# A new written order for the first tile's jobs, and other engines for the signs of six weight chunks

## Chip, core and metric

The kernel runs on one core of one Trainium2 chip. The metric is the device time of one execution in microseconds (us). Before the change it is 944.29 us, the median of 3 runs (944.16 to 944.9).

## What is computed

Pooled attention, then a gated feed-forward layer on its output. Batch 8, 8 heads, 576 positions, head size 64; k and v are averaged over groups of 8 positions, so that 72 keys are left.

```python
k_p = k.reshape(B, H, Sp, pool, D).mean(axis=3)          # pool = 8, Sp = 72
v_p = v.reshape(B, H, Sp, pool, D).mean(axis=3)
scores = scale * np.matmul(q, k_p.transpose(0, 1, 3, 2))
attn = softmax(scores)
x = (attn @ v_p), heads joined: 4608 tokens x 512
g = x @ w_gate                                            # 512 x 1536, float64 weights
out = (g / (1 + exp(-g)) * (x @ w_val)) @ w_out           # 1536 x 512
```

q, k and v are float32, the three weights float64.

## The kernel before, in words

The 4608 tokens are cut into nine tiles of 512. For a tile the feed-forward runs over 12 chunks of 128 hidden units: a gate product (G), a value product (V), tanh and gating on ScalarE and VectorE, and a projection (O) of twelve matmuls into four PSUM banks that collect all chunks. Each float32 operand is split into a high and a low part, so that three cheap matmuls stand for one exact product. From the second tile on a planner places the work by costs and due times. The first tile has an order written out by hand, and the change is about that order.

`first_tile` (L1134) goes through the names in `ORDER` (L38 to L55) and calls one job for each. Every engine executes its instructions in program order, so what `ORDER` sets is, for each engine, the sequence of its own jobs; across engines only the data and the buffers bind. The projection of the last step and the stores of the tile's output stand outside the written part; the compiler places them. A name is letters and a number. The number is a chunk of weights, a batch (0 or 1), a piece of tokens or a step.

Transfers (all from SyncE's queue, SP in the profile): Lk and Lr bring k of batch 0 and 1, Lv and Lu bring v, Lq a piece of q, Lw a chunk of weights (L209), La inputs of batch 2, T a transposition of a piece's weights (L717), through the same queue.

Attention for pieces 0 to 8 (four of the first tile, five of the second; pieces 4 and 8 have 64 tokens): S scores (TensorE), M the scores less their maximum (VectorE, L620), E exponentials (ScalarE), Na the inverse sums (VectorE), N the product with them (GpSimd), H and P the high and low half for the transposition (ScalarE, GpSimd), T, Y the product with v (TensorE), X and Z its high and low part (ScalarE, VectorE), which are the tile's x.

Sums of v: Vp and Vq (TensorE), Vm, Vo, Vs its scale (VectorE, TensorE, VectorE), R the ratios (VectorE), Vx (ScalarE), Vh, Vg (VectorE), Vf (ScalarE) its parts. Sums of k: Kp on VectorE, Kb and Kq on GpSimd.

Weights: a chunk lies as 128 x 1536 float64 numbers in a buffer, of which there are two, shared with the first k. It is turned into float32 by integer work on its halves: a shifts the low words (L215, VectorE), b puts the sign beside them (L219), c takes the magnitude of the high words (L231, ScalarE), d joins all (L235, VectorE) and so frees the buffer for the chunk after next. Then e sums (ScalarE), f (TensorE) and g (VectorE) give a scale, h and j the high halves (ScalarE), i and k the low ones (VectorE), l and m the output weights (ScalarE, GpSimd), un a table of factors (GpSimd).

Steps 0 to 14: steps 0 to 2 are chunks 0 to 2 on the tile's first 256 tokens, steps 3 to 5 the same chunks on the other 256, steps 6 to 14 chunks 3 to 11 on all 512. G and V are twelve matmuls each (L903 to L905), t the tanh (L917), u the gating (L921), v the product with the value (L927), w and y the high and low part of the result, O the projection (L939). One PSUM bank serves all G of this tile and one all V, so that G of a step waits for u of the step before, and V for y. D and ZERO are matmuls with zeros that fill time.

`w_sign` is where the second part of the change lies. Before it there are two ways: for the chunks in `SIGN_AS_INT` an integer AND on VectorE (L225), for the others a float multiplication by 2^-60 on ScalarE that leaves a signed zero (L227).

Of the kernel before, what the change touches and what calls it, by code (L numbers as in the profile page):

```python
# [14 lines left out]
ALU = mybir.AluOpType  # L15
# [19 lines left out]


ORDER = """
Lk0 Lq0 Lk1 Lv2 Lv1 Lv0 Lq1 Lw0 Kp0 Kb0 Kp1 CZ Lw1 Lr0 Lu0 S0 Vp0 M0 Lq2 Vp2 E0 Na0 S1  # L38
a0 N0 b0 Vp1 Lq3 M1 Vm0 a1 Vo0 E1 Vs0 Kq0 R0 Vx0 H0 Vh0 Vq0 b1 Vg0 S2 Lr1 Na1 Lu2 P0 S3
Lq4 Vf0 M2 N1 T0 Lq5 H1 Kq1 Vq2 E2 c0 Y0 Lu1 Na2 X0 d0 Z0 Lw2 P1 l0 Vq1 e0 M3 T1 m0 f0  # L40
c1 N2 g0 ZERO Vm1 h0 Vo1 E3 d1 H2 j0 Vs1 Lw3 P2 e1 R1 D10 Y1 Vg1 Vx1 T2 a2 X1 l1 Vh1 un0
b2 m1 Z1 D8 f1 g1 k0 S4 i0 a3 G0 h1 Lq6 j1 M4 un1 c2 V0 k1 t0 Y2 E4 d2 b3 Lw4 i1 Na3 u0
l2 N3 D8 G1 v0 X2 w0 c3 y0 m2 Z2 O0 t1 d3 H3 V1 e2 u1 Lw5 P3 v1 l3 f2 g2 e3 T3 a4 h2 f3
j2 g3 un2 i2 w1 j3 y1 h3 k2 D4 O1 b4 i3 G2 k3 a5 V2 b5 t2 Y3 c4 u2 m3 X3 v2 Vf1 Z3 d4 G3
w2 c5 y2 Lw6 un3 t3 O2 l4 d5 e4 V3 u3 Lw7 m4 l5 f4 G4 v3 g4 w3 m5 y3 j4 O3 e5 k4 V4 Na4
t4 c6 u4 N4 f5 G5 v4 g5 h4 w4 a6 S5 H4 y4 t5 un5 b6 i4 V5 Lq7 u5 P4 M5 O4 G6 v5 T4 un4
a7 w5 c7 y5 d6 E5 O5 t6 j5 u6 Lw8 S6 e6 k5 Na5 V6 h5 Lq8 M6 l6 N5 H5 i5 f6 G7 v6 E6 P5
g6 w6 h6 y6 j6 T5 a8 O6 t7 u7 un6 Na6 c8 S7 b8 b7 V7 M7 i6 G8 E7 v7 d7 w7 Y4 y7 Lw9 N6
e7 O7 t8 d8 H6 X4 u8 Lw10 m6 Y5 e8 Z4 V8 l8 k6 X5 m8 l7 Z5 c9 f7 f8 v8 m7 G9 g7 w8 g8 j7
un7 y8 j8 un8 a9 h7 V9 t9 Na7 b9 u9 N7 O8 v9 i7 k7 w9 H7 y9 G10 k8 c10 d9 h8 V10 t10  # L50
Lw11 i8 e9 u10 La0 a10 l9 f9 O9 v10 m9 g9 w10 h9 y10 j9 un9 O10 i9 b10 k9 La1 a11 G11
b11 d10 V11 t11 Pa0 l10 u11 e10 G12 v11 w11 y11 c11 m10 f10 O11 g10 t12 d11 h10 j10 u12
l11 un10 V12 k10 e11 i10 m11 La2 G13 v12 P6 w12 y12 f11 O12 t13 g11 P7 T6 u13 h11 j11 T7
k11 S8 Ln i11 un11 Pa2 V13 M8 La3 E8 G14 La4 Na8 v13 N8 w13 y13 Y6 Pa3 t14 u14 V14 X6
Pa4 H8 La5 P8 O13 v14 La6 w14 T8 y14 Z6 Pa5 Y7 Pa6 Y8 X7 Z7 X8 La7 Pa1 Z8 Pa7 A A  # L55
"""
# [36 lines left out]
def attention_then_swiglu(  # L93
# [125 lines left out]
    def w_sign(c):  # L219


        ws, high = chunks[c]["ws"], chunks[c]["high"]
        if c in SIGN_AS_INT:
            sign = ws.bitcast(U16)
            nc.vector.tensor_single_scalar(sign[:, :, 1], sign[:, :, 3], 0x8000, ALU.bitwise_and)  # L225
        else:
            nc.scalar.activation(  # L227
                ws.bitcast(F16)[:, :, 1], high.bitcast(F32), AF.Copy, scale=2.0**-60
            )
# [904 lines left out]
    def first_tile():  # L1134
# [360 lines left out]
```

## Time and profile before

| | |
|---|---|
| median of 3 runs | 944.29 us |
| the profiled execution | 944.47 us, its span 942.5 us |
| TensorE busy | 911.6 us, 97% of the span |
| VectorE, ScalarE, GpSimd busy | 635.5, 493.5, 415.1 us |
| share of TensorE in the chain that ended last | 91% |
| first tile | the first 171 us or so of the span |

The profile is of one execution. PE is TensorE, PEld its weight load, DVE VectorE, ACT ScalarE, POOL GpSimd, SP SyncE's queue, on which all transfers are issued. A timeline row gives start and length in us, engine, line, operation, output and input, and in brackets how long the engine idled before and what released it. As each engine runs in program order, a row is matched with a job's name by counting along the order.

### The profile page before, as it was taken

The page shows a single profiled execution, that of the slowest core. Times are in us where ns is not written, and L with a number is a line of the kernel's source. Part 1 is how long each engine was busy: PE and PEld are TensorE (multiplying, and loading weights), DVE is VectorE, ACT ScalarE, POOL GpSimd, SP SyncE. Part 2 cuts the span into 40 slices and gives each one's busy share as a digit, 9 for nine tenths or more (in the row PEclk, how much of TensorE's full clock was granted, in tenths as well). Part 3 has the DMA queues.
Part 4 walks back from the last instruction along what each step waited for, and adds up shares of the span by engine and source line. Part 5 has one row for each costly group of instructions (what it writes and reads, how often), then busy time and mean ns, then how long its engine had stood idle before and what let it go on. Part 6 is the DMA issues. An engine that isn't in the chain of part 4 may idle for free.

```text
span 942.5 us, 16833 instructions
## 1 busy us (share of the span) xinstructions
PE 911.6 (97%) x6512; PEld 590.5 (63%) x6512; DVE 635.5 (67%) x1145; ACT 493.5 (52%) x971; POOL 415.1 (44%) x483
## 2 busy tenths in 40 slices
PE   5789999899999999999999999999999999999997
PEld 4567545455555576567657775776577757765775
DVE  5788877787786767676866678777854584345232
ACT  2899884264555454656365545472556554323232
POOL 4533427289747854687265442562123421120111
PEclk9899999999999999999999999999999999999999
DMA  9865634346425551654155525741322332001001
GB/s 349 247 169 186 188 134 127 111 135 199 93 75 138 159 113 30 182 132 135 29 151 148 128 51 153 182 94 27 88 59 63 74 67 57 12 1 45 1 1 46
DMA packets 155536, 103.18 MB, mean 109 GB/s; under 512 B 113216, under 2 KB 141888, under 8 KB 153920
## 3 DMA queue, kind: packets, MB, share of 16 engines
q1 hardware_dynamic: 155456, 102.11, 39.2%
q8 instruction: 51, 0.84, 0.4%
q14 instruction: 29, 0.24, 0.1%
HBM read 67.63 MB, written 9.44 MB: 82 GB/s over the span
## 4 chain that ended last, share of the span: by engine, by line
PE 91%; DMA 3%; DVE 2%; ACT 1%; POOL 1%; issue 1%; SPq 0%; POOLq 0%; DVEq 0%; ACTq 0%
PE acc L939 30%; PE gv L1036 28%; PE gv L903 9%; PE gv L904 9%; PE gv L905 9%; DMA kr<-k_rows 1%; PE ps L616 1%; DMA pt<-half 1%; PE ps L740 1%; PE ps L617 1%; PE ps L741 1%; DMA k<-k_rows 1%; DMA in<-q_rows 1%; PE ps L610 1%; ACT ws L227 0%
## 5 line engine op out<-in xcount | busy, mean ns | idle before, releaser
L1306 POOL TENSOR_TENSOR hl<-hf,hh 128x512 bf16<-128x512 f32 x69 | 91.3, 1323 | 235.7 <-ACT hh L1300 235.7
L917 ACT ACTIVATE hf<-gv,un 128x512 f32<-128x512 f32 (+1 forms) x111 | 74.9, 675 | 213.4 <-PE gv L1036 145.3
L939 PE MATMUL acc<-hh,wo_l 128*128 128x512 bf16 (+1 forms) x444 | 169.2, 383 | 0.0
L939 PE MATMUL acc<-hl,wo_h 128*128 128x512 bf16 (+1 forms) x444 | 166.1, 376 | 0.4 <-POOL hl L1306 0.2
L903 PE MATMUL gv<-x,wgv_h 128*128 128x512 f16 (+1 forms) x432 | 158.8, 368 | 3.7 <-ACT x L751 1.9
L904 PE MATMUL gv<-x,wgv_h 128*128 128x512 f16 (+1 forms) x432 | 158.6, 367 | 1.3 <-DVE x L755 1.3
L905 PE MATMUL gv<-x,wgv_l 128*128 128x512 f16 (+1 forms) x432 | 158.6, 367 | 0.5 <-DVE wgv_l L268 0.5
L921 DVE SCALAR_TENSOR_TENSOR hf<-hf,gv 128x512 f32<-128x512 f32 (+1 forms) x111 | 74.2, 669 | 109.4 <-ACT hf L917 108.9
L939 PE MATMUL acc<-hh,wo_h 128*128 128x512 f32 (+1 forms) x444 | 130.5, 416 | 0.6 <-ACT hh L1300 0.4
L599 POOL TENSOR_TENSOR box<-qt,box 64x512 f16<-64x512 f32 (+1 forms) x60 | 68.9, 1149 | 119.2 <-ACT box L598 98.7
L1036 PEld LDWEIGHTS <-mixed 128*128 128x128 f16 x1026 | 99.1, 98 | 26.6 <-issue 1.5
L1036 PEld LDWEIGHTS <-wgv_h 128*128 128x128 f16 x912 | 87.8, 98 | 32.5 <-issue 1.9
L1300 ACT CAST hh<-hf 128x512 fp32r<-128x512 f32 x69 | 42.7, 618 | 115.3 <-DVE hf L927 115.3
L1036 PE MATMUL gv<-xc,mixed 128*128 128x256 f16 x684 | 93.2, 272 | 0.0
L939 PEld LDWEIGHTS acc<-hh,wo_h 128*128 128x128 f32 x444 | 76.7, 190 | 14.8 <-ACT hh L1300 0.9
L1036 PE MATMUL gv<-xc,wgv_h 128*128 128x256 f16 x456 | 80.7, 272 | 1.3 <-DVE gv L1385 1.3
L1036 PE MATMUL gv<-x,wgv_h 128*128 128x256 f16 x456 | 80.8, 273 | 0.0
L927 DVE SCALAR_TENSOR_TENSOR hf<-gv,un,hf 128x512 f32<-128x512 f32 x69 | 51.5, 746 | 39.1 <-PE gv L1036 35.7
L939 PEld LDWEIGHTS <-wo_h 128*128 128x128 bf16 x444 | 43.4, 98 | 53.9 <-issue 27.3
L905 PEld LDWEIGHTS <-wgv_l 128*128 128x128 f16 x432 | 42.2, 98 | 48.4 <-issue 1.8
L904 PEld LDWEIGHTS <-wgv_h 128*128 128x128 f16 x432 | 42.2, 98 | 45.1 <-issue 4.4
L903 PEld LDWEIGHTS <-wgv_h 128*128 128x128 f16 x432 | 42.7, 99 | 41.4
(170 smaller groups left out, 1791.5 us busy)
## 6 DMA issues: line engine op xcount, KB each, us to landing
ws<-w_all SPq DMA_DIRECT2D x12, 1536.0 KB, 7.4
qt<-q_twice SPq DMA_DIRECT2D x48, 256.0 KB, 2.9
out_t<-ob SPq DMA_DIRECT2D x36, 256.0 KB, 2.3
in<-k_rows SPq DMA_DIRECT2D x12, 576.0 KB, 4.7
in<-q_rows SPq DMA_DIRECT2D x12, 576.0 KB, 4.8
in<-v_main SPq DMA_DIRECT2D x12, 512.0 KB, 5.0
in<-v_rest SPq DMA_DIRECT2D x12, 512.0 KB, 4.9
qt<-q_rows SPq DMA_DIRECT2D x8, 256.0 KB, 3.9
```

What stands on the lines that cost most here:

```text
L599: nc.gpsimd.tensor_sub(o[rows], qt[rows], o[rows])
L610: nc.tensor.matmul(o, qt[rows, j, :n], ksum[b][rows, j], start=True, stop=True)
L903: nc.tensor.matmul(o, wh, x["h"][:, j, a:e], start=(j == 0), stop=False)
L904: nc.tensor.matmul(o, wh, x["l"][:, j, a:e], start=False, stop=False)
L905: nc.tensor.matmul(o, wl, x["h"][:, j, a:e], start=False, stop=(j == NJ - 1))
L917: nc.scalar.activation(hf, gate, AF.Tanh, scale=un[:, c, 0:1])
L921: nc.vector.scalar_tensor_tensor(out=hf, in0=hf, scalar=1.0, in1=gate, op0=ALU.add, op1=ALU.mult)
L927: nc.vector.scalar_tensor_tensor(out=out, in0=val, scalar=un[:, c, 2:3], in1=hf, op0=ALU.mult, op1=ALU.mult)
L939: nc.tensor.matmul(acc[j][:, a:e], w[:, c, j * P : (j + 1) * P], h[:, :n], start=begin and at < NJ, stop=end and w is wo_l,)
L1036: nc.tensor.matmul(o, a, b, start=begin and j + n == 0, stop=j == HJ - 1 and n == 2, skip_group_check=True,)
L1300: nc.scalar.copy(hh[:, :n], hf)
L1306: eng.tensor_sub(hl[:, :n], hf, hh[:, :n].bitcast(F32))
```

## The change

It touches `ORDER`, which keeps its 469 names and moves some, and `w_sign`.

```diff
-Lk0 Lq0 Lk1 Lv2 Lv1 Lv0 Lq1 Lw0 Kp0 Kb0 Kp1 CZ Lw1 Lr0 Lu0 S0 Vp0 M0 Lq2 Vp2 E0 Na0 S1
-a0 N0 b0 Vp1 Lq3 M1 Vm0 a1 Vo0 E1 Vs0 Kq0 R0 Vx0 H0 Vh0 Vq0 b1 Vg0 S2 Lr1 Na1 Lu2 P0 S3
-Lq4 Vf0 M2 N1 T0 Lq5 H1 Kq1 Vq2 E2 c0 Y0 Lu1 Na2 X0 d0 Z0 Lw2 P1 l0 Vq1 e0 M3 T1 m0 f0
-c1 N2 g0 ZERO Vm1 h0 Vo1 E3 d1 H2 j0 Vs1 Lw3 P2 e1 R1 D10 Y1 Vg1 Vx1 T2 a2 X1 l1 Vh1 un0
-b2 m1 Z1 D8 f1 g1 k0 S4 i0 a3 G0 h1 Lq6 j1 M4 un1 c2 V0 k1 t0 Y2 E4 d2 b3 Lw4 i1 Na3 u0
-l2 N3 D8 G1 v0 X2 w0 c3 y0 m2 Z2 O0 t1 d3 H3 V1 e2 u1 Lw5 P3 v1 l3 f2 g2 e3 T3 a4 h2 f3
-j2 g3 un2 i2 w1 j3 y1 h3 k2 D4 O1 b4 i3 G2 k3 a5 V2 b5 t2 Y3 c4 u2 m3 X3 v2 Vf1 Z3 d4 G3
...
-l11 un10 V12 k10 e11 i10 m11 La2 G13 v12 P6 w12 y12 f11 O12 t13 g11 P7 T6 u13 h11 j11 T7
-k11 S8 Ln i11 un11 Pa2 V13 M8 La3 E8 G14 La4 Na8 v13 N8 w13 y13 Y6 Pa3 t14 u14 V14 X6
-Pa4 H8 La5 P8 O13 v14 La6 w14 T8 y14 Z6 Pa5 Y7 Pa6 Y8 X7 Z7 X8 La7 Pa1 Z8 Pa7 A A
+Lv2 Lk0 Lq0 Lk1 Lv1 Lv0 Lq1 Lw0 Kp0 Kb0 Kp1 CZ Lw1 Lr0 Lu0 S0 Vp2 M0 Lq2 E0 Na0 S1 a0
+Vp0 N0 b0 Vp1 Lq3 M1 Vm0 Vo0 H0 a1 Lr1 E1 Vs0 Kq0 R0 Vx0 Vh0 Vq0 b1 Vg0 S2 Na1 Lu2 P0 S3
+Lq4 Vf0 M2 N1 T0 Kq1 H1 Vq2 E2 c0 Y0 Na2 Lu1 X0 Lq5 d0 Z0 Lw2 P1 l0 Vq1 e0 N2 M3 T1 m0
+Vm1 f0 c1 g0 ZERO d1 H2 j0 Vo1 Vs1 Lw3 P2 a2 e1 h0 D10 Y1 Vg1 Vx1 X1 R1 E3 T2 l1 Vh1 b2
+m1 Z1 D8 f1 g1 k0 S4 i0 a3 h1 c2 j1 M4 un1 V0 G0 un0 i1 k1 b3 t0 Y2 E4 d2 Lw4 Na3 u0 N3
+D8 G1 l2 v0 X2 w0 c3 y0 m2 Z2 O0 e2 d3 H3 V1 t1 u1 Lw5 P3 v1 f2 g2 e3 T3 a4 h2 f3 j2 g3
+un2 w1 l3 k2 j3 h3 y1 Lq6 i2 D4 i3 G2 k3 a5 b4 V2 b5 t2 c4 u2 Y3 m3 X3 Vf1 v2 Z3 d4 O1
+G3 w2 c5 y2 Lw6 un3 t3 O2 d5 e4 V3 l4 u3 Lw7 m4 l5 f4 G4 v3 g4 w3 m5 e5 y3 j4 O3 V4 Na4
...
+e11 u12 l11 un10 k10 i10 m11 La2 v12 P6 w12 y12 f11 G13 t13 g11 P7 La3 T6 u13 j11 T7 h11
+k11 S8 Ln i11 un11 Pa2 V13 M8 E8 G14 O12 La4 v13 w13 V14 Na8 y13 Y6 Pa3 t14 N8 Pa4 H8
+La5 X6 O13 u14 v14 P8 La6 w14 T8 Pa5 Y7 y14 Z6 X7 Pa6 Z7 Y8 X8 La7 Pa1 Z8 Pa7 A A
-SIGN_AS_INT = (5, 8, 11)
+SIGN_AS_INT = (2, 4, 8, 9)
+SIGN_ON_POOL = (5, 11)
...
-        if c in SIGN_AS_INT:
+        if c in SIGN_ON_POOL:
+            nc.gpsimd.tensor_single_scalar(
+                ws.bitcast(F16)[:, :, 1], high.bitcast(F32), 2.0**-60, ALU.mult
+            )
+        elif c in SIGN_AS_INT:
```

In the lines left out, between step 3 and step 12, TensorE's sequence is the same but for f7 and f8, and b9 goes in front of u9 on VectorE. The signs of chunks 2, 4 and 9 go from ScalarE to VectorE, those of 5 and 11 from VectorE to GpSimd; chunk 8 stays on VectorE, 0, 1, 3, 6, 7 and 10 on ScalarE.

More of the change, by code (lines that the diff above doesn't have):

```diff
@@ L44 @@
-j2 g3 un2 i2 w1 j3 y1 h3 k2 D4 O1 b4 i3 G2 k3 a5 V2 b5 t2 Y3 c4 u2 m3 X3 v2 Vf1 Z3 d4 G3
[L45 to L49, printed above, removed]
@@ L50 @@
-un7 y8 j8 un8 a9 h7 V9 t9 Na7 b9 u9 N7 O8 v9 i7 k7 w9 H7 y9 G10 k8 c10 d9 h8 V10 t10
-Lw11 i8 e9 u10 La0 a10 l9 f9 O9 v10 m9 g9 w10 h9 y10 j9 un9 O10 i9 b10 k9 La1 a11 G11
-b11 d10 V11 t11 Pa0 l10 u11 e10 G12 v11 w11 y11 c11 m10 f10 O11 g10 t12 d11 h10 j10 u12
-l11 un10 V12 k10 e11 i10 m11 La2 G13 v12 P6 w12 y12 f11 O12 t13 g11 P7 T6 u13 h11 j11 T7
-k11 S8 Ln i11 un11 Pa2 V13 M8 La3 E8 G14 La4 Na8 v13 N8 w13 y13 Y6 Pa3 t14 u14 V14 X6
-Pa4 H8 La5 P8 O13 v14 La6 w14 T8 y14 Z6 Pa5 Y7 Pa6 Y8 X7 Z7 X8 La7 Pa1 Z8 Pa7 A A
@@ new lines @@
+un2 w1 l3 k2 j3 h3 y1 Lq6 i2 D4 i3 G2 k3 a5 b4 V2 b5 t2 c4 u2 Y3 m3 X3 Vf1 v2 Z3 d4 O1
+G3 w2 c5 y2 Lw6 un3 t3 O2 d5 e4 V3 l4 u3 Lw7 m4 l5 f4 G4 v3 g4 w3 m5 e5 y3 j4 O3 V4 Na4
+k4 t4 c6 u4 f5 G5 v4 w4 g5 h4 a6 N4 S5 H4 y4 t5 un5 b6 i4 V5 Lq7 u5 P4 M5 O4 G6 v5 T4
+un4 a7 w5 y5 d6 E5 t6 O5 j5 u6 Lw8 S6 e6 Na5 V6 M6 h5 k5 Lq8 l6 N5 i5 f6 c7 G7 H5 g6 v6
+w6 y6 P5 T5 t7 a8 O6 u7 E6 un6 c8 h6 Na6 S7 b8 b7 V7 M7 G8 E7 v7 d7 w7 Y4 j6 y7 Lw9 N6
+O7 t8 d8 Lw10 H6 i6 X4 e7 u8 m6 Y5 e8 Z4 V8 X5 l8 k6 m8 l7 m7 Z5 c9 f8 f7 v8 G9 g7 a9 g8
@@ new lines @@
+un7 w8 y8 j8 un8 h7 V9 t9 j7 Na7 b9 u9 N7 O8 v9 i7 k7 w9 H7 y9 G10 k8 c10 d9 a10 h8 V10
+t10 Lw11 i8 e9 u10 La0 l9 f9 O9 v10 m9 g9 w10 y10 j9 b10 un9 h9 O10 i9 La1 a11 G11 b11
+d10 V11 t11 Pa0 l10 u11 e10 G12 v11 w11 y11 c11 m10 f10 k9 O11 g10 t12 V12 h10 d11 j10
+e11 u12 l11 un10 k10 i10 m11 La2 v12 P6 w12 y12 f11 G13 t13 g11 P7 La3 T6 u13 j11 T7 h11
+k11 S8 Ln i11 un11 Pa2 V13 M8 E8 G14 O12 La4 v13 w13 V14 Na8 y13 Y6 Pa3 t14 N8 Pa4 H8
+La5 X6 O13 u14 v14 P8 La6 w14 T8 Pa5 Y7 y14 Z6 X7 Pa6 Z7 Y8 X8 La7 Pa1 Z8 Pa7 A A
```

## The prediction

> **What bounds the kernel now.** I read the windows first, to find where TensorE is not the bound at all. The change touches the first tile alone, whose last projection lies near 168 us.
>
> ```profile
> core 0 of [0], span 942.5 us
> core 0: us, PE busy (x) PEld busy (x) DVE busy (x) ACT busy (x) POOL busy (x), PEclk, DMA share, GB/s
> 0.00:80.00 80.00, 57.85 (x457) 47.22 (x458) 59.52 (x122) 59.41 (x92) 34.68 (x52) 0.94 0.77 245
> 80.00:160.00 80.00, 79.98 (x493) 44.98 (x491) 64.71 (x108) 61.82 (x97) 33.84 (x43) 1.00 0.49 159
> 160.00:180.00 20.00, 17.56 (x116) 9.24 (x115) 16.36 (x26) 5.10 (x11) 5.80 (x9) 1.00 0.56 163
> ```
>
> Columns: length, then busy time (and instructions) of each engine, granted clock, DMA share, GB/s. From 80 to 160 us TensorE is busy for 79.98 of 80.00: nothing that the other engines do earlier can shorten that stretch, only a new wait can lengthen it. TensorE stands idle for 80.00 − 57.85 = 22.15 us in the first 80 and for 2.44 in the last window. These 24.6 us are all that an order can win. Second, the waits of TensorE up to 83 us:
>
> ```profile
> PE ps L610 <- DVE spare L282: 8.0, 2, 7.0
> PE ps L728 <- DMA pt<-half: 3.0, 2, 2.2
> ```
>
> The 8.0 us are the wait for k at the very start, the 3.0 two waits for transposed weights; the rest is smaller pieces. Third, the timeline of TensorE at the seam between the first and the second tile:
>
> ```profile
> 169.44 0.19 PE L728 MATMUL ps<-pt,spare 128*128 128x64 f16 x1 [0.53 <-DMA pt<-half]
> 171.16 0.38 PE L903 MATMUL gv<-x,wgv_h 128*128 128x512 f16 x1 [1.08 <-ACT x L751]
> 172.37 0.38 PE L904 MATMUL gv<-x,wgv_h 128*128 128x512 f16 x1 [0.83 <-DVE x L755]
> ```
>
> These three are the whole 2.44 = 0.53 + 1.08 + 0.83: piece 8's transposed weights land late (Y8), so X8 and Z8 are late, and the second tile's first matmuls wait for them.
>
> **Start, 0 to 48 us.** Lv2 ahead of Lk0 puts 512 KB before k: at the first window's 245 GB/s that is up to 2.1 us, by which S0 and Lw1 come later. I cost this at nothing: the bytes asked for up to S2 are the same, and Vq0 and S2 wait for batch 1's v, the last of them, which no job moves forward. If that cover failed it would cost up to its 2.1 us. From S2 on the path is M2, E2, c0, d0, then Lw2, whose buffer d0 frees:
>
> ```profile
> 29.12 0.46 DVE L627 TENSOR_TENSOR sc<-ps,mx 128x288 f32<-128x288 f32 x1
> 30.02 0.70 ACT L634 ACTIVATE sc<-sc 128x576 f32<-128x576 f32 x1
> 32.33 1.71 DVE L237 SCALAR_TENSOR_TENSOR mixed<-mixed,ws 128x1536 uint32<-128x1536 uint32 x1
> 34.07 0.33 SPq L212 DMA_DIRECT2D ws<-w_all  x1
> ws<-w_all SPq DMA_DIRECT2D x1, 1536.0 KB, 7.5
> ws<-w_all SPq DMA_DIRECT2D x1, 1536.0 KB, 6.3
> ```
>
> The last two rows are the landings of chunk 2 and of the chunk issued near 74.6 us, in us from issue. M2 ends at 29.12 + 0.46 = 29.58, E2 starts only at 30.02, since H0 (now moved up, in front of E1) stood before b1 on ScalarE. E2 follows M2 at once in the new order: d0 and Lw2 come 0.4 to 0.5 earlier, Lw2 at 33.6, and chunk 2 lands at 33.6 + 7.5 = 41.1. That gain is taken back, because a2 now stands in front of R1, Vg1, Vh1 on VectorE and b2 is new there:
>
> ```profile
> 39.81 0.84 DVE L883 TENSOR_TENSOR top<-p2s 128x1 f32<-128x1 f32 x1
> 42.21 0.96 DVE L217 TENSOR_SCALAR ws<-ws 128x1536 uint32<-128x1536 uint32 x1
> 43.26 0.98 DVE L436 SCALAR_TENSOR_TENSOR spare<-ps,inv,spare 64x256 f16<-64x256 f32 x2
> 44.57 0.75 DVE L755 SCALAR_TENSOR_TENSOR x<-ps,r,x 128x512 f16<-128x512 f32 x1 [0.33 <-ACT x L751]
> 47.60 0.16 DVE L202 TENSOR_SCALAR p2w<-ps 128x2 uint32<-128x2 uint32 x1 [2.28 <-PE ps L197]
> 68.69 1.90 DVE L225 TENSOR_SCALAR ws<-ws 128x1536 uint16<-128x1536 uint16 x1
> 44.94 3.65 ACT L227 ACTIVATE ws<-ws 128x1536 f16<-128x1536 f32 x1
> ```
>
> Rows one to four are R1 (with Vg1 up to the next row: 42.21 − 39.81 = 2.40), a2, Vh1, Z1; the fifth is g1, today held by TensorE (f1); the last two are a sign on VectorE (1.90) and on ScalarE (3.65). In the new order VectorE has idled since Vs1 and begins a2 at 41.1; 41.1 + 0.96 + 2.40 + 0.98 + 1.90 + 0.75 = 48.1, or 47.6 if each start-to-start step is the 0.1 shorter that these rows overlap. g1 was at 47.60. So 1.9 us of work fill a wait of 2.28 and g1 moves by 0 to +0.5; f1 is no longer the holder. What ScalarE saves by losing b2 goes into b3, which now stands ahead of t0: it isn't late for u0, as VectorE's jobs from g1 to u0 are the same. Queued behind a2's wait are R1, Vg1, Vh1, b2, Z1 and g1, all in this sum.
>
> **48 to 76 us.** From g1 to d3 every VectorE job keeps its length, so d3 keeps its place, and with it Lw5 and behind that T3 and Y3:
>
> ```profile
> 58.97 1.76 DVE L237 SCALAR_TENSOR_TENSOR mixed<-mixed,ws 128x1536 uint32<-128x1536 uint32 x1 [0.44 <-ACT mixed L233]
> pt<-half SPq DMA_TRANSPOSE x1, 8.3
> 70.34 0.22 PE L728 MATMUL ps<-pt,spare 128*128 128x128 f16 x1
> 72.97 0.27 PE L904 MATMUL gv<-x,wgv_h 128*128 128x256 f16 x1 [0.52 <-DVE x L755]
> ```
>
> d3 frees chunk 5's buffer; T3's data queue behind chunk 5 and take 8.3 us; Y3 starts at 70.34 with TensorE just free. G2 and V2 now run before Y3 and O1 after it. H3 is now behind e2 on ScalarE, so P3 and T3 are issued up to 0.4 later; their data wait behind chunk 5 anyhow, which hides it (0 to +0.4). Ahead of Y3 TensorE then waits about 1.2 us with nothing to do; behind it O1 (twelve matmuls) covers X3 and Z3, which today cost the 0.52 of the last row and a wait of like size before it. One replaces the other, and G3 ends where it did. Sum of the first 76 us: +0.2, between −0.8 (chunk 2 landing in the 6.3 us of the later row, with some 0.4 of the 1.2 lost again at f1) and +0.9 (0.5 + 0.4).
>
> One thing could add to this, the half clock:
>
> ```profile
> 60.78:64.19 3.41, 1.67 (x10) 1.06 (x10) 2.58 (x8) 3.41 (x9) 3.29 (x5) 1.00 0.73 213
> 64.19:67.60 3.41, 3.20 (x15) 2.33 (x15) 3.05 (x5) 3.41 (x5) 0.93 (x3) 0.52 0.99 292
> ```
>
> A window of 3.41 us in which TensorE worked only 1.67 is followed by one at 0.52. In the new order 64.19 to 67.60 holds G2 after a wait for i2; were it counted as idle, the next window would be slow too, V2 would end after Y3's data have landed, and some 0.8 us be lost. By the Trainium skill (TensorE: Matmul & The Clock Gate, the section on HAM oscillation) only an idle gap beyond about 3.4 us drops the clock; by it this loss has no chance, but the trace shows a drop after a window that was half busy, so I keep it.
>
> **The signs.** Moves of b4, b8, b9 onto VectorE cost 1.90 each there and free 3.65 on ScalarE for chunks 2, 4 and 9. b4 takes the slot of b5, so VectorE is level around 69 us; b9 stands before u9 and v9, in a stretch in which TensorE has two groups of twelve and a projection queued, so 1.9 is covered; if the cover were gone it would be at most that. For chunks 5 and 11 GpSimd runs an operation that no row shows. Nearest rows:
>
> ```profile
> L1306 POOL TENSOR_TENSOR hl<-hf,hh 128x512 bf16<-128x512 f32 x69 | 91.3, 1323 | 235.7 <-ACT hh L1300 235.7
> 9.68 0.52 POOL L186 MEMSET zeros<- 128x512 f16 x1
> 75.13 1.76 DVE L237 SCALAR_TENSOR_TENSOR mixed<-mixed,ws 128x1536 uint32<-128x1536 uint32 x1 [0.22 <-ACT mixed L233]
> ```
>
> A two-input pass costs 1323 ns for 512 elements, 3.97 us for 1536; a memset 0.52 for 512, 1.56 for 1536. I take 3 us: one input, but read and written in strides, so between them and nearer the tensor row. b5 can start where it starts today on VectorE, at 68.69, and d5 (last row) needs it at 75.13: 6.4 us of slack. Behind it on GpSimd stand m3 and un3, idle until then. It costs nothing below 6.4 us; above, each us holds VectorE at d5, with u3 and v3 queued behind, and TensorE's G4 behind u3. b11 has more room: c11, d11 and Pa0 behind it come late in the tile.
>
> **The queue of transfers.** Lu1 goes ahead of Lq5 and so lands up to 1 us sooner (256 KB at 245 GB/s), which Vq1 can't pass on, since Y1 waits for T1. Lq6 goes behind T3, far ahead of S6. La3 goes ahead of T6 and T7 and waits for the buffer that Pa0 frees; Pa0 stands before P6 on GpSimd anyway, so T6 isn't held. All three at nothing; the cover of each is the job named, and if La3's buffer came late, T6 and Y6 would wait as long.
>
> **The seam.** Here the order moves most: f11 before G13, O12 from before S8 to behind G14, Pa3 before N8, H8 before X6, Y6 behind V14. TensorE's sum is the same, only permuted. Rows of piece 8 (S8, Na8, H8, P8, T8, the landing):
>
> ```profile
> 150.11 1.18 PE L939 MATMUL acc<-hh,wo_h 128*128 128x512 f32 x4
> 152.99 0.72 PE L610 MATMUL ps<-spare,qt 64*64 64x72 f32 x16
> 156.59 0.74 DVE L655 TENSOR_REDUCE sm<-sc 64x8 f32<-64x576 f32 x1 [0.81 <-ACT sc L634]
> 157.91 1.14 POOL L664 TENSOR_TENSOR sc<-sc,ri 64x576 f32<-64x576 f32 x1 [3.50 <-DVE ri L660]
> 160.53 0.60 ACT L677 CAST half<-sc 64x512 f16<-64x512 f32 x1
> 162.10 1.16 POOL L683 TENSOR_TENSOR half<-sc,half 64x512 f16<-64x512 f32 x1
> 163.55 1.25 SPq L719 DMA_TRANSPOSE pt<-half  x1
> pt<-half SPq DMA_TRANSPOSE x1, 5.8
> ```
>
> S8 starts 2.9 us earlier, at 150.1 (O12's 152.99 − 150.11). On VectorE u13, k11 and i11 still stand before M8 and wait for t13, j11, h11, so I pass on 1.1 of the 2.9 (bounds 0 and 2.9): Na8 at 155.5. N8 follows as today, 1.3 later, at 156.8, for 1.14. H8 doesn't wait for Y6 and X6 any more: 158.0 instead of 160.53. P8 follows H8's copies at 158.9 instead of 162.10, as Pa3 is done by then (La3 is issued before T6 and landed long since). T8 comes 1.45 behind P8's start, as today: 160.3 instead of 163.55. With 5.8 us to land, Y8's data are there at 166.1; today they come at 169.44, 0.53 after TensorE has ended O14, so at 168.9 it has them in hand. So the 0.53 goes. If the compiler puts Y8 before O14 (which it may, since O14 lies outside the written order), X8 and Z8 hide under O14, and the whole 2.44 goes. If O14 stays first, X8 and Z8 still follow Y8 with nothing over them, about 1.1 us stay, and 1.3 goes. I take 1.9, the middle, as nothing in the trace decides it.
>
> **Sum.** +0.2 − 1.9 = −1.7. The profiled execution took 944.47 (span 942.5, 1.97 around it), 0.18 over the median of the three runs, 944.29. On the median: 944.29 − 1.7 = 942.6.
>
> **Rivals.**
>
> Nothing is won at the seam (16%): the copies of the first tile's output stand between X7 and X8 on ScalarE and between Z7 and Z8 on VectorE, and move along. For it: X8 and Z8 cost 1.08 and 0.83 today, Y8 only 0.53. Against: T8's 3.2 us. Then +0.2 alone: 944.5.
>
> The opening wins too (16%): VectorE's chain from a2 begins earlier because chunk 2 lands sooner; Y1 and f1 come 0.4 earlier with T1. Then −0.8 − 1.9, at best −0.8 − 2.44: 941.1 to 941.6.
>
> The GpSimd sign is slow (8%), the one that ends on the other side. Price: each us beyond 6.4 is lost at G4. From 8.1 us on it eats up the 1.7, from 10.0 the kernel is slower by over 0.2%; 10.5 us give 944.29 − 1.7 + 4.1 = 946.7. Against it: 10.0 is over twice the dearest neighbour, 3.97. The Trainium skill (GPSIMD Engine Reference, section on instruction dispatch) gives about 6 us for the first call of a freshly loaded routine. If that held for b5, whose kind of operation is new on this engine, it would by estimate last 9 us and the kernel take 945.2; no run here shows such a load.
>
> The half clock falls on V2, or the transposes come late (6%): +0.8, 943.4.
>
> **How the numbers follow.** The forecast has 54%, with a range of its own from 942.0 to 943.2 (the seam's 2.44 to 1.3). About 0.2% (1.9 us) is what a measurement of this kernel can tell from no change; 942.4 is the border, inside the forecast's own range. Faster: 0.42 of the forecast's 54 as 26, and the 16 of the opening: 42%. Slower by more: a slow sign and unseen waits in the 80 us that are full now, 10%. The same: 48%. The range leaves out half of the slow sign and the best of the opening: 940.9 to 945.2.
>
> **What would show it.** Right: VectorE's L217 for chunk 2 begins at about 41 behind a wait for its transfer; g1 within 0.5 of 47.6; Y3 near 70.4 with a wait before it and none at G3; T8 near 160; at the seam at most 1.1 us of waits in place of 2.44. Wrong: a GpSimd sign over 6.4 us with VectorE waiting for it at L237; a half clock between 67.6 and 71; a wait of TensorE between 80 and 160 us; g1 before 47 or behind 48.5.

## The result, and the profile after

The changed kernel takes 949.74 us (median of 9 runs, 947.4 to 950.97). The kernel before, run beside it on the same chips, took 947.27 in the median of its 9 runs. The ratio of the runs compared is 1.0038, with a 95% interval of 1.0023 to 1.0054: 3.6 us slower, by 2.2 to 5.1. (The two medians alone would give 1.0026.) The forecast was 942.6, in a range of 940.9 to 945.2, worked out from a time before of 944.29; from there, a ratio of 1.0038 would give 947.9, outside the range too. The profiled execution took 949.19 us with a span of 947.4, 4.9 more than the 942.5 of before. Behind L217 the line numbers are 1 to 5 higher than before (the join d was L237 and is L242); L225 is now the GpSimd sign and L230 VectorE's.

The windows of the changed kernel, to be held against the three of before (columns as there):

```profile
core 0: us, PE busy (x) PEld busy (x) DVE busy (x) ACT busy (x) POOL busy (x), PEclk, DMA share, GB/s
0.00:80.00 80.00, 56.85 (x434) 47.08 (x435) 62.20 (x117) 50.65 (x84) 43.02 (x52) 0.89 0.77 233
80.00:160.00 80.00, 76.26 (x469) 43.60 (x473) 63.13 (x105) 58.65 (x97) 42.75 (x45) 1.00 0.47 157
160.00:180.00 20.00, 19.84 (x122) 10.84 (x126) 16.20 (x25) 6.52 (x13) 8.16 (x11) 0.91 0.76 194
```

At the seam the waits went, as forecast: 160 to 180 us has 0.16 us of idle TensorE instead of 2.44. But the stretch that was full, 80 to 160, now has 80.00 − 76.26 = 3.7 us without work, and the granted clock is 0.91 behind it. (This profile has 6414 matmuls and that of before 6512, so some records may be missing; the waits below don't depend on that.) TensorE's largest waits up to 83 us, and its two waits between 140 and 180:

```profile
PE ps L615 <- DVE spare L287: 8.6, 2, 8.1
PE ps L733 <- DMA pt<-half: 2.2, 2, 1.3
PE acc L944 <- DVE hl L1205: 2.0, 1, 2.0
```

```profile
157.66 0.38 PE L908 MATMUL gv<-x,wgv_h 128*128 128x512 f16 x1 [1.24 <-DVE hf L926]
160.02 0.39 PE L910 MATMUL gv<-x,wgv_l 128*128 128x512 f16 x1 [1.77 <-DVE wgv_l L273]
```

The wait of 2.0 us on hl stands at O2, 77.15 us; before it was 0.2. The waits of 1.24 and 1.77 us are new. Both places lie behind a sign on GpSimd. The first, as VectorE (DVE) and GpSimd (POOL) ran it:

```profile
69.13 7.61 POOL L225 TENSOR_SCALAR ws<-ws 128x1536 f16<-128x1536 f32 x1 [5.54 <-DVE ws L218]
78.05 1.71 POOL L1215 TENSOR_TENSOR p2w<-p2w 128x1 f32<-128x1 f32 x1
68.95 1.90 DVE L230 TENSOR_SCALAR ws<-ws 128x1536 uint16<-128x1536 uint16 x1
73.20 3.57 DVE L242 SCALAR_TENSOR_TENSOR mixed<-mixed,ws 128x1536 uint32<-128x1536 uint32 x1
76.69 0.41 DVE L1205 TENSOR_TENSOR hl<-gv,hh 128x256 bf16<-128x256 f32 x1
77.02 2.68 DVE L242 SCALAR_TENSOR_TENSOR mixed<-mixed,ws 128x1536 uint32<-128x1536 uint32 x1
79.63 0.41 DVE L926 SCALAR_TENSOR_TENSOR hf<-hf,gv 128x256 f32<-128x256 f32 x1
```

The sign of chunk 5 took 7.61 us, not 3. And d4, which needs nothing of chunk 5, took 3.57 us instead of 1.75 and ended at 76.77, within 0.03 of the sign's end at 76.74. So y2 (76.69) came 2.2 later than the 74.49 of before, and O2 waited for it. d5 took 2.68 instead of 1.76, and u3 (79.63) came 2.8 late.

The second place, with chunk 11's sign:

```profile
138.36 7.71 POOL L225 TENSOR_SCALAR ws<-ws 128x1536 f16<-128x1536 f32 x1 [6.15 <-DVE ws L218]
146.67 2.33 POOL L292 TENSOR_TENSOR in<-in 128x512 f32<-128x512 f32 x1
156.57 0.20 POOL L1215 TENSOR_TENSOR p2w<-p2w 128x1 f32<-128x1 f32 x1
156.81 0.20 DVE L1350 TENSOR_TENSOR un<-p2w,mt 128x36 f32<-128x36 f32 x1 [3.85 <-POOL p2w L1215]
156.92 0.68 DVE L926 SCALAR_TENSOR_TENSOR hf<-hf,gv 128x512 f32<-128x512 f32 x1
157.52 2.44 DVE L273 SCALAR_TENSOR_TENSOR wgv_l<-mixed,sw,wgv_h 128x512 f16<-128x512 f32 x2
```

Again 7.7 us. Everything behind it on GpSimd moves: the first key sum of Pa0 from 137.86 to 146.67, the product of chunk 11's factors (L1215) to 156.57. For that product VectorE waits 3.85 us at the second tile's table of factors (L1350), and behind it in its program stand the hf and the two low parts for which TensorE waits.

Where the 4.9 us arose in these two profiles is read from TensorE's first matmul of a few groups, before and after: V3 75.85 and 78.04 (+2.2), S5 83.29 and 86.31 (+3.0), V12 144.57 and 147.19 (+2.6), the second tile's first scores 174.84 and 179.66 (+4.8), and from there on the shift stays within 0.1. Between the last two are 3.0 us of new waits, 2.4 us of old ones gone, and a stretch at a granted clock of 0.60 from 160 to 164 (1.6 us): +2.2 in all.

### The profile page after: what moved, and what is told of

It is laid out like the page before. It is cut to its first block, busy times and chain, and to the rows that moved or that the text cites. A ratio compares the mean times of both kernels' runs of the same rounds, so it can differ in the third digit from the quotient of the medians.

```text
span 947.4 us, 16735 instructions
## 1 busy us (share of the span) xinstructions
PE 908.0 (96%) x6414; PEld 593.1 (63%) x6512; DVE 641.0 (68%) x1146; ACT 483.4 (51%) x968; POOL 432.3 (46%) x485
## 4 chain that ended last, share of the span: by engine, by line
PE 88%; DMA 4%; DVE 4%; POOL 1%; issue 1%; ACT 1%; SPq 0%; POOLq 0%; DVEq 0%; ACTq 0%
PE acc L944 29%; PE gv L1041 27%; PE gv L908 9%; PE gv L910 8%; PE gv L909 8%; DMA pt<-half 1%; DMA vr<-v_main 1%; DMA ws<-w_all 1%; DVE mixed L242 1%; PE ps L621 1%; PE ps L745 1%; PE ps L615 1%; PE ps L622 1%; PE ps L746 1%; DVE wgv_l L273 1%
## 5 line engine op out<-in xcount | busy, mean ns | idle before, releaser
L910 PE MATMUL gv<-x,wgv_l 128*128 128x512 f16 (+1 forms) x432 | 160.6, 372 | 3.6 <-DVE wgv_l L273 3.6
L908 PE MATMUL gv<-x,wgv_h 128*128 128x512 f16 (+1 forms) x432 | 160.6, 372 | 2.9 <-DVE hf L926 2.9
L944 PE MATMUL acc<-hl,wo_h 128*128 128x512 bf16 (+1 forms) x418 | 155.4, 374 | 6.6 <-DVE hl L1205 2.0
L909 PE MATMUL gv<-x,wgv_h 128*128 128x512 f16 (+1 forms) x432 | 160.4, 371 | 0.0
L926 DVE SCALAR_TENSOR_TENSOR hf<-hf,gv 128x512 f32<-128x512 f32 (+1 forms) x111 | 74.3, 670 | 108.3 <-ACT hf L922 107.8
L944 PE MATMUL acc<-hh,wo_l 128*128 128x512 bf16 (+1 forms) x372 | 140.5, 380 | 1.8 <-issue 0.3
L932 DVE SCALAR_TENSOR_TENSOR hf<-gv,un,hf 128x512 f32<-128x512 f32 x69 | 51.5, 746 | 39.1 <-PE gv L1041 35.7
```

The lines of the kernel that those rows point to most:

```text
L908: nc.tensor.matmul(o, wh, x["h"][:, j, a:e], start=(j == 0), stop=False)
L909: nc.tensor.matmul(o, wh, x["l"][:, j, a:e], start=False, stop=False)
L910: nc.tensor.matmul(o, wl, x["h"][:, j, a:e], start=False, stop=(j == NJ - 1))
L926: nc.vector.scalar_tensor_tensor(out=hf, in0=hf, scalar=1.0, in1=gate, op0=ALU.add, op1=ALU.mult)
L932: nc.vector.scalar_tensor_tensor(out=out, in0=val, scalar=un[:, c, 2:3], in1=hf, op0=ALU.mult, op1=ALU.mult)
L944: nc.tensor.matmul(acc[j][:, a:e], w[:, c, j * P : (j + 1) * P], h[:, :n], start=begin and at < NJ, stop=end and w is wo_l,)
```

## The experiments

The sign theory: the two GpSimd signs cause both losses, at O2 and at 157 to 160 us. The rival, the order theory: the new order makes them, and the signs stand there by chance. The numbers of the experiments are those of their labels (there is no 3). Ratios are to the kernel before on the same chip, with 95% intervals.

**1, no sign on GpSimd.**

```diff
-SIGN_AS_INT = (2, 4, 8, 9)
-SIGN_ON_POOL = (5, 11)
+SIGN_AS_INT = (2, 4, 5, 8, 9, 11)
+SIGN_ON_POOL = ()
```

> The new order with no sign on GpSimd: chunks 2, 4, 5, 8, 9 and 11 on VectorE, the rest on ScalarE. Sign theory (the two GpSimd signs of 7.61 and 7.71 us cause both losses): TensorE's wait at the second accumulation (2.0 us at 76 us) and its two waits of 1.24 and 1.77 us at 157 to 160 us go, and with the latter the half-clock stretch of about 1.7 us behind them; the removed seam waits (2.4 us) stay removed. Time 2 to 3 us below before, ratio 0.997 to 0.998. Order theory (the new order itself makes these waits): ratio stays at 1.003 to 1.005. If VectorE is now too full (1.9 us more in each of two places), the ratio falls between, near 1.000.

Measured: 943.66 us, ratio 0.9978 (0.9963 to 0.9994). Faster than before, as the sign theory had it. (Its profiled execution took 946.9, 3.2 over the median, most of it in the opening: V3 begins at 79.87, in experiment 11's profile at 77.58.) TensorE's waits at 157 to 160 us are gone and the one at O2 is 0.16.

**2, the old order with the new signs.** Only the ORDER block is that of before.

> The old order with the new placing of the signs (2, 4, 8, 9 on VectorE, 5 and 11 on GpSimd). Sign theory: the waits near 77 us and behind chunk 11 come in the old order too, and the three seam waits of 2.4 us stay: 4 to 7 us above before, ratio 1.004 to 1.008, with GpSimd signs of 7.6 us again. Order theory: about the time before, ratio 0.999 to 1.002.

Measured: 949.39 us, ratio 1.0042 (1.0027 to 1.0057). So the signs cost some 4 us without the new order too: TensorE waits 1.09 us at O2 and 2.05 at 144.08, and the seam's 1.08 and 0.83 stay. Here chunk 10's join met chunk 11's sign (POOL, then DVE):

```profile
137.21 6.19 POOL L225 TENSOR_SCALAR ws<-ws 128x1536 f16<-128x1536 f32 x1 [4.00 <-DVE ws L218]
137.79 5.64 DVE L242 SCALAR_TENSOR_TENSOR mixed<-mixed,ws 128x1536 uint32<-128x1536 uint32 x1 [0.66 <-ACT ws L232]
```

The join took 5.64 us and ended at 143.43, with the sign at 143.40.

**4 and 5, one sign each on GpSimd.** 4: SIGN_ON_POOL = (11,), chunk 5 on VectorE; 5: SIGN_ON_POOL = (5,), chunk 11 on VectorE.

> The new order with only chunk 11's sign on GpSimd, chunk 5's on VectorE. Sign theory: the loss near 77 us goes (2.2 us at the third value step, 3.0 us by the fifth score step), the loss of 3.0 us and the half clock of 1.7 us at 157 to 166 us stay: about 3 us below the changed kernel, 1 to 2 us above before, ratio 1.001 to 1.003. Order theory: as the changed kernel, 1.003 to 1.005. VectorE's join of chunk 4 takes 1.75 us again under either if the GpSimd sign beside it stretched it, 3.57 us if something else did.

> The new order with only chunk 5's sign on GpSimd, chunk 11's on VectorE. Sign theory: the loss near 77 us stays with the join of chunk 4 at about 3.6 us, the waits of 1.24 and 1.77 us and the half clock at 157 to 166 us go: 4 to 5 us below the changed kernel, about the time before or 1 us below it, ratio 0.999 to 1.001. Order theory: as the changed kernel, 1.003 to 1.005.

Measured: 946.99 us, ratio 1.0014 (0.9997 to 1.0030), and 945.74 us, ratio 1.0001 (0.9987 to 1.0016). Against experiment 1, chunk 11's sign costs 0.36% (3.4 us) and chunk 5's 0.23% (2.2 us); together 0.59%, and the changed kernel stands 0.60% above experiment 1. The two losses add up to the whole, as well as intervals of some 0.15% to either side can tell. The join of chunk 4 in 4 and in 5:

```profile
75.46 1.75 DVE L242 SCALAR_TENSOR_TENSOR mixed<-mixed,ws 128x1536 uint32<-128x1536 uint32 x1
```

```profile
73.28 3.58 DVE L242 SCALAR_TENSOR_TENSOR mixed<-mixed,ws 128x1536 uint32<-128x1536 uint32 x1
```

1.75 us without the GpSimd sign beside it, 3.58 with it. V3's place alone would not show chunk 5's loss. In the profiles of the new order without a GpSimd sign there (experiments 1, 4, 8, 10 and 11) V3 begins at 77.58 to 79.87, against 78.04 in the changed kernel's and 78.14 in experiment 5's, since all that leads up to Y3 ran later in them: Y3 begins at 72.06 to 73.73, against 70.71 and 70.79. Counted from Y3, V3 comes 7.3 us later in the changed kernel and in 5, and 5.5 to 6.4 in those five.

In 4 both waits at 157 to 160 stand again, but no half clock behind them (1.00 from 156 to 180), so those 1.6 us of the changed kernel's profile don't come with every execution.

**6, the seam alone.** The old ORDER up to V12, k10 and e11, the new one behind them; the signs of before.

```diff
 d11 h10 j10 u12 l11 un10 V12 k10 e11
-i10 m11 La2 G13 v12 P6 w12 y12 f11 O12 t13 g11 P7 T6 u13 h11 j11 T7
+i10 m11 La2 v12 P6 w12 y12 f11 G13 t13 g11 P7 La3 T6 u13 j11 T7 h11
...
```

> The old order up to the twelfth value step, the new order behind it, and the signs of before (5, 8, 11 on VectorE, the rest on ScalarE): only the seam between the first and the second tile is changed. If the prediction's seam term is right (TensorE's three waits of 0.53, 1.08 and 0.83 us go, at most some tenths stay): 1.3 to 2.4 us below before, ratio 0.9975 to 0.9986, and no half clock between 155 and 175 us. If the gain of the first experiment came from the opening or from the sign of chunks 2, 4 and 9 on VectorE: ratio 0.999 to 1.001.

Measured: 942.44 us, ratio 0.9969 (0.9956 to 0.9982). The seam gives 2.9 us (1.7 to 4.2). In its profile TensorE has no wait above 0.2 us between 80 and 440 us; the few behind that (1.3 us at 442, 0.4 and 0.2 at 933 and 934) are in the profile of before too.

**7, what the sign costs by itself.** Experiment 1's kernel with added work behind the last output, where all engines are idle.

```diff
...
+        pool(a["ws"].bitcast(F16)[:, :, 1], a["high"])
+        w_join(0)
+        pool(a["wf"].bitcast(F16)[:, :n], a["high"])
+        few(a["wf"].bitcast(U32)[:, :64])
+        pool(b["ws"].bitcast(F16)[:, :, 1], b["high"])
+        w_join(0)
+        pool(a["ws"].bitcast(F16)[:, :, 1], a["high"])
+        for _ in range(3):
+            w_shift(1)
+        few(a["low"][:, :64])
+        sign = b["ws"].bitcast(U16)
+        nc.vector.tensor_single_scalar(sign[:, :, 1], sign[:, :, 3], 0x8000, ALU.bitwise_and)
+        pool(a["ws"].bitcast(F16)[:, :, 1], a["high"])
+        pool(mixed[:, 2 * n : 3 * n].bitcast(F16)[:, :n], b["wf"])
```

The lines left out load and shift two chunks. `pool` is GpSimd's multiplication by 2^-60, `w_join` and `w_shift` are VectorE's join and shift, `few` is a VectorE shift of 64 columns, there to set the order. GpSimd's six are: the sign alone; into contiguous output; the sign with a join beside it; with three shifts; begun beside VectorE's sign; contiguous on both sides.

> The first experiment's kernel with a few instructions added behind the last output, which change no output and add some 40 us to the time: GpSimd signs of the form used (128x1536, float32 read and float16 written, each 8 bytes apart) alone, beside a VectorE join, beside VectorE shifts (one input), and behind a VectorE sign; the same multiply into contiguous float16; and from contiguous into contiguous. Port theory (the join, with two inputs in SBUF, and a GpSimd instruction exclude each other): the sign alone 4.5 us; beside the join 6.2 us, and the join as long as what is left of the sign; beside the shifts 4.5 us again. Own-cost theory (the strided sign takes 7.6 us by itself): 7.6 us alone, and the join beside it 1.75 us. A contiguous write is near 3.9 us if the 8-byte step costs little, or near half of the strided one if the step costs as it seems to on ScalarE (3.66 us against 1.62).

GpSimd's six, then VectorE's four beside or between them:

```profile
951.44 6.14 POOL L1451 TENSOR_SCALAR ws<-ws 128x1536 f16<-128x1536 f32 x1 [16.04 <-DVE ws L218]
959.46 4.14 POOL L1451 TENSOR_SCALAR mixed<-ws 128x1536 f16<-128x1536 f32 x1 [1.88 <-DVE mixed L242]
963.67 6.14 POOL L1451 TENSOR_SCALAR ws<-ws 128x1536 f16<-128x1536 f32 x1
969.99 6.79 POOL L1451 TENSOR_SCALAR ws<-ws 128x1536 f16<-128x1536 f32 x1 [0.18 <-DVE mixed L242]
978.79 7.50 POOL L1451 TENSOR_SCALAR ws<-ws 128x1536 f16<-128x1536 f32 x1 [2.00 <-DVE ws L1454]
986.37 4.08 POOL L1451 TENSOR_SCALAR mixed<-mixed 128x1536 f16<-128x1536 f32 x1
957.61 1.76 DVE L242 SCALAR_TENSOR_TENSOR mixed<-mixed,ws 128x1536 uint32<-128x1536 uint32 x1 [6.26 <-POOL ws L1451]
963.85 5.98 DVE L242 SCALAR_TENSOR_TENSOR mixed<-mixed,ws 128x1536 uint32<-128x1536 uint32 x1
969.85 8.75 DVE L218 TENSOR_SCALAR ws<-ws 128x1536 uint32<-128x1536 uint32 x3
978.63 1.87 DVE L1467 TENSOR_SCALAR ws<-ws 128x1536 uint16<-128x1536 uint16 x1
```

Neither theory had the number. Alone the sign takes 6.14 us; the join that waits for it begins 0.03 us behind its end. Into contiguous output the same multiply takes 4.14, and 4.08 from contiguous input: reading every 8 bytes costs nothing, writing 2 bytes in every 8 costs 2.0 us. Beside it:
- The join, begun 0.18 us behind the sign, took 5.98 us instead of 1.76 and ended 0.02 us behind it; the sign stayed at 6.14.
- Three shifts took 8.75 us together. The first began 0.14 ahead of the sign, which took 6.79 and ended at 976.78; the group ended at 978.60, so that the other two, at 0.9 each (the L217 row of before has 0.96), fit in behind the sign.
- The sign begun 0.16 us behind VectorE's sign took 7.50 instead of 6.14.

So the sign and VectorE's weight steps (shift, sign, join) hold each other up: the one begun first delays the other. The Trainium skill has a rule of this kind (SBUF — State Buffer, section "SBUF: two separate sides"): VectorE and GpSimd share a pair of ports, an exclusive lock that goes to whichever starts first, a VectorE operation with two SBUF inputs or in a two-port mode, or a GpSimd operation, for its whole length. The shifts agree with it (whether they run in such a mode, no row shows). The join agrees in that it was held, but not in how long: one blocked up to 969.81 would have ended at about 971.6, not at 969.83. Why it ended with the sign stays open.

The changed kernel's rows follow: 6.14 + 1.47 = 7.61 for chunk 5, begun 1.7 us before VectorE's sign of chunk 4 ended; 6.14 + 1.57 = 7.71 for chunk 11, begun 1.58 before the join of chunk 10 ended.

**8, the queue behind chunk 11's sign.** Experiment 4 with Pa0 later on GpSimd.

```diff
-d10 V11 t11 Pa0 l10 u11 e10
+d10 V11 t11 l10 u11 e10
...
-k11 S8 Ln i11 un11 Pa2
+k11 S8 Ln i11 un11 Pa0 Pa2
```

> The fourth experiment (chunk 11's sign on GpSimd) with the 4.8 us of key sums that GpSimd does right behind that sign moved behind the last p2w step of the first tile. Queue theory (the loss at 157 to 166 us is GpSimd's p2w of chunk 11, which comes out of its queue 3.7 us late): that p2w is done at about 153 to 154 us instead of 156.8, TensorE's waits of 1.24 and 1.77 us shrink to under 0.5 us and the half clock behind them goes, 3 to 4 us below the fourth experiment, ratio 0.997 to 0.999. If the late join of chunk 11 itself holds TensorE, they stay and the ratio is again 1.001 to 1.002.

Measured: 950.56 us, ratio 1.0061 (1.0047 to 1.0074), a miss. TensorE's first two waits here behind 80 us:

```profile
158.25 0.39 PE L910 MATMUL gv<-x,wgv_l 128*128 128x512 f16 x1 [1.50 <-DVE wgv_l L273]
172.97 1.41 PE L944 MATMUL acc<-hh,wo_h 128*128 128x512 f32 x4 [2.50 <-ACT hh L1201]
```

The product of the factors was done at 154.5, 2.2 us earlier than in experiment 4, and the wait of 1.24 went. But the two low parts now ran beside the moved key sums (2.96 us, 2.44 in 4, 1.87 before the change). And SyncE's queue stood until 158.9 us for the buffer that Pa0 frees (151.4 in the changed kernel), with the next k behind it, for whose sums VectorE waited 6.02 us ahead of step 14's products: 2.50 us of TensorE at 172.97.

**9, work on GpSimd that nobody waits for.** Experiment 1 with one multiply added beside chunk 5's weights.

```diff
+        if c == 5:
+            nc.gpsimd.tensor_single_scalar(
+                scratch, high.bitcast(F32), 2.0**-60, ALU.mult
+            )
```

> The first experiment's kernel (all signs as there) with one GpSimd multiply added at the place of chunk 5's sign, which reads the same data and writes contiguous float16 into a buffer that nobody reads: no instruction waits for its result but the buffer's reuse. Port theory: the join of chunk 4 (1.75 us) is stretched as far as the two overlap, and the signs of VectorE beside it delay the GpSimd multiply in turn; if it reaches to the join, TensorE waits at the second accumulation again, 0.5 to 2 us above the first experiment, ratio 0.998 to 1.000. Late-data theory (only d5's wait for the sign costs time): the join stays at 1.75 us and the ratio at 0.997 to 0.999.

Measured: 951.15 us, ratio 1.0063 (1.0048 to 1.0078), 0.85% above experiment 1 (8 us): far more than either theory had, on the side of the ports. GpSimd, VectorE, TensorE:

```profile
69.54 4.95 POOL L226 TENSOR_SCALAR scratch<-ws 128x1536 f16<-128x1536 f32 x1 [4.15 <-DMA ws<-w_all]
74.56 2.62 POOL L287 TENSOR_TENSOR wo_l<-mixed,wo_h 128x512 bf16<-128x512 f32 x1
77.14 1.80 POOL L1220 TENSOR_TENSOR p2w<-p2w 128x1 f32<-128x1 f32 x1
70.36 8.54 DVE L235 TENSOR_SCALAR ws<-ws 128x1536 uint16<-128x1536 uint16 x2
79.20 0.40 PE L913 MATMUL gv<-x,wgv_h 128*128 128x256 f16 x1 [4.57 <-DVE hf L931]
```

VectorE's signs of chunks 4 and 5 (3.64 us in experiment 1) took 8.54, 4.9 more, and the small steps behind them, u2 and Z3 among them, came that much late; TensorE waited 4.57 and 0.88 us, and ran at a clock of 0.50 from 80 to 84 us. No data of the added multiply was needed by anyone, and the buffer that it reads was not free before d5 ended, at 84.1 us, 9.6 behind the multiply's end. GpSimd's m3 took 2.62 instead of 1.27, and the one-column product behind it 1.80 instead of 0.19, ending 0.04 us behind VectorE: they were held in turn.

**10, the factors of chunk 11 on VectorE.** Experiment 4, with the two small products (L1215, L1216) on VectorE for chunk 11.

```diff
-            nc.gpsimd.tensor_mul(p2w[:, c, 2:3], p2w[:, c, 0:1], p2w[:, c, 1:2])
-            nc.gpsimd.tensor_mul(kept["un"][:, c], p2w[:, c], xs[0]["mt"])
+            eng = nc.vector if c == 11 else nc.gpsimd
+            eng.tensor_mul(p2w[:, c, 2:3], p2w[:, c, 0:1], p2w[:, c, 1:2])
+            eng.tensor_mul(kept["un"][:, c], p2w[:, c], xs[0]["mt"])
```

> The fourth experiment (chunk 11's sign on GpSimd) with the two small products of chunk 11 (p2w and un) moved from GpSimd to VectorE, behind the two low weight parts there. Queue theory (VectorE's un of the second tile waits 3.85 us for GpSimd's p2w, with the tanh product of the 14th value step and two low weight parts behind it, and TensorE waits 1.24 and 1.77 us for those): both TensorE waits go, 3 us below the fourth experiment, ratio 0.997 to 0.999. Port theory alone (what costs is that GpSimd's sign holds VectorE's join back): the waits stay, ratio 1.000 to 1.002.

Measured: 948.13 us, ratio 1.0033 (1.0019 to 1.0047), a miss. The waits of 1.24 and 1.77 are gone, as the queue theory said; others took their place:

```profile
162.99 0.38 PE L908 MATMUL gv<-x,wgv_h 128*128 128x512 f16 x1 [1.32 <-DVE hl L1205]
172.87 0.38 PE L944 MATMUL acc<-hl,wo_h 128*128 128x512 bf16 x1 [1.00 <-DVE hl L1205]
```

With smaller ones of 0.36, 0.28 and 0.56 they make 3.5 us, in place of the 3.4 of experiment 4 (1.24, 1.77 and 0.39). So the factors were only the first thing that came late. GpSimd's whole program behind the sign is still late (the first key sum at 146.6), and VectorE waits 3.18 us ahead of 166.11 for the next rows of k; that the new waits all go back to this was not traced row by row. What would win back chunk 11's 3.4 us with the sign kept on GpSimd was not found.

**11, the new order alone.** SIGN_AS_INT = (5, 8, 11) as before, in the new order.

> The new order with the signs of before (5, 8, 11 on VectorE, the rest on ScalarE). If the new order's gain is the seam and its opening is neutral: 2 to 3 us below before, ratio 0.9968 to 0.998. If the new opening needs chunk 2's and chunk 4's signs on VectorE: ScalarE has 3.66 us more ahead of the softmax and weight parts of two chunks, 1 to 3 us of waits between 40 and 72 us, ratio 0.999 to 1.001.

Measured: 944.64 us, ratio 0.9999 (0.9985 to 1.0013). With the same signs experiment 6 has 0.9969, so the new order ahead of the seam costs about 0.3% (2.8 us); the two intervals only just don't overlap. From the profiles of 6 and 11: V3 at 76.90 and 77.58, S5 at 84.34 and 85.32, V12 at 145.49 and 147.44, the second tile's scores at 172.76 and 175.44. How much of the first 0.7 is the order stays open, as the same opening has V3 at 75.85 in the profile of before and at 76.90 in that of 6. Between S5 and V12 it is a wait that experiment 6 doesn't have:

```profile
141.69 0.38 PE L908 MATMUL gv<-x,wgv_h 128*128 128x512 f16 x1 [1.08 <-ACT wo_h L279]
```

**12, the seam with VectorE's signs.** Experiment 6's order, experiment 1's signs.

> The sixth experiment (old opening, new tail) with chunk 2's, 4's and 9's signs too on VectorE (2, 4, 5, 8, 9, 11; none on GpSimd). If taking 3.66 us of ScalarE per sign for 1.9 us of VectorE helps in the old opening as it did in the new one (2 us between the eleventh and the first experiment): 1 to 2 us below the sixth, ratio 0.995 to 0.996. If it only mended what the new opening had made late: as the sixth, 0.996 to 0.998. If VectorE becomes the late one in the old opening: 0.998 to 1.000.

Measured: 942.73 us, ratio 0.9958 (0.9940 to 0.9975): not told apart from experiment 6. This and 6 are the versions that beat both kernels; 0.9969 means 2.9 us under the kernel before.

## Why the prediction failed

**The step that failed is "I take 3 us" for the GpSimd sign, with bounds of 1.56 and 3.97.** The instruction takes 6.14 us alone and 7.6 to 7.7 in its place. The bound came from a contiguous output. So the first term that was mis-sized is this instruction, by 3.1 us alone and by 4.6 to 4.7 in its place. The trace of before had rows that warned of it: ScalarE's sign took 3.65 us, and its magnitude of as many elements, which reads the same words and writes contiguous float32 (L233), 1.62. By that factor, 2.25, a GpSimd pass of 3.97 would have been 8.9 us: too much, as the factor on GpSimd is 6.14 / 4.14 = 1.48, but beyond the 6.4 of slack.

**"It costs nothing below 6.4 us" failed too, and weighed as much.** By that step 7.61 us would have cost 1.2 at d5. It cost 2.2 (0.23%, experiment 5 against 1), because the sign held d4, which it feeds nothing, and what followed on GpSimd held d5. Slack counted along the data was the wrong measure: experiment 9 lost 8 us to a GpSimd instruction whose result nobody used. The trace of before shows the mechanism where I read past it; chunk 11's join there, and GpSimd's product of three columns, mostly 0.2 us:

```profile
142.23 1.76 DVE L237 SCALAR_TENSOR_TENSOR mixed<-mixed,ws 128x1536 uint32<-128x1536 uint32 x1
142.47 1.58 POOL L1211 TENSOR_TENSOR un<-p2w,mt 128x3 f32<-128x3 f32 x1
```

The product took 1.58 us and ended at 144.05, 0.06 behind the join.

**"b11 has more room" failed.** Chunk 11's join had room; GpSimd's program behind the sign had none. It cost more than chunk 5's (0.36% against 0.23%).

**The seam, −1.9 between −1.3 and −2.44: right in size, at the far end, but not by the transfer.** TensorE waits 0.16 there instead of 2.44, and experiment 6 measures −2.9 (−1.7 to −4.2) for it alone. The sign of being right that was set for it, T8 near 160 us, did not come: T8 was issued at 170.38 in the changed kernel and at 163.49 in experiment 6, against 163.55 before (V12, ahead of it, stands 0.9 later in 6 than before, so T8 came about 1.0 earlier, not 3.2). What took the waits away is one of the two branches that the prediction left open when it took their middle: Y8 now stands inside O14. From experiment 6:

```profile
167.82 0.39 PE L944 MATMUL acc<-hl,wo_h 128*128 128x512 bf16 x1
168.05 0.19 PE L733 MATMUL ps<-pt,spare 128*128 128x64 f16 x1
168.53 0.39 PE L944 MATMUL acc<-hh,wo_l 128*128 128x512 bf16 x1
```

The first and the last are O14, and the rest of O14 covers X8 and Z8. That the compiler would place it so was luck.

**The opening, +0.2 between −0.8 and +0.9: mostly right in its marks, too small in its size.** In the changed kernel a2 began at 40.51 (41.1 forecast, but with no wait before it) and g1 at 47.42 (47.6 to 48.1), Y3 at 70.71 (70.4) with a wait before it, and G3 waited for nothing. But the whole order ahead of the seam costs about 2.8 us with the old signs (experiment 11 against 6) and with VectorE's signs 1.9 (0.9978 against 0.9958, with intervals that overlap); some of it is the wait of 0.8 to 1.1 us that experiments 1, 5, 9 and 11 show at 142 to 149 us, in a stretch of which I said that only a new wait could lengthen it, and then looked for none. What makes it was not followed further.

**The half clock on V2** (6%) did not decide: the clock was 0.65 from 64 to 68 us and 0.92 from 68 to 72, but Y3 still waited 0.90 us for its data. In the profiles of experiments 1, 4 and 10 it did come, with a clock of 0.50 to 0.53 from 68 to 72 us, over V2, and Y3 behind it had nothing left to wait for; what that cost was not separated.

**The transfers at nothing: right.** T6 was issued at 155.28, as its GpSimd half ended (155.25), so La3 didn't hold it; in experiment 8, where Pa0 came late, it did.

**The signs on VectorE at nothing:** in the seam-only order it made no difference that can be measured (6 and 12); in the new order it gave 0.2% (11 and 1), with intervals that overlap.

**The rival on the other side** was the right one, with 8%, and its mechanism half right: a slow sign, but charged only through d5 and from 6.4 us on. The 6 us that the Trainium skill (GPSIMD Engine Reference, instruction dispatch) gives for the first call of a freshly loaded kernel did not show: in experiment 7 the first such multiply of the program and a later one beside a join took 6.14 us each.

**The chances.** "0.42 of the forecast's 54 as 26" is a slip: it is 23, so that "faster" would have had 39%, not 42. The outcome, slower by more than 0.2%, had 10%.

## What to carry to other kernels

Before work is moved to GpSimd beside a busy VectorE, ask what it excludes there, not only when its result is due: look in the trace for small GpSimd instructions that grow and end together with a VectorE instruction. Price a strided write from a strided write, on whatever engine has one, by the factor to its contiguous neighbour. And behind a long instruction count the whole program of its engine as late: taking away the first wait that this causes (experiments 8 and 10) only brought up the next.

## What the runs showed of the hardware

- A GpSimd multiply of 128 x 1536, float32 to float16: 4.08 us contiguous, 4.14 with input every 8 bytes, 6.14 with output every 8 bytes too.
- A GpSimd instruction and VectorE's shift, sign or join hold each other up. Of three shifts of 0.96 us beside a sign two ended only behind it (8.75 together); joins of 1.75 us begun beside a sign took up to 5.98 and ended within 0.03 us of its end, without making it longer (6.14 with and without). GpSimd products of 0.2 us took up to 1.8 and ended within 0.06 of VectorE's.
- VectorE's hf and gv of chunk steps (L926 and L932, one input in PSUM) beside a GpSimd sign kept their length: 0.46 and 0.49 us at 70.6 and 71.2 us, beside the first sign.
- The same waits brought a half clock in one profiled execution (0.60 from 160 to 164 us, the changed kernel) and none in another (experiment 4).
